# A gated linear attention with an MLP: gates loaded with each chunk's steps turned by one row, and the carried angle added on VectorE

## The chip, the core and the metric

The kernel runs on one core of a Trainium2 chip. The metric is the device time of one execution in microseconds, as the median of several runs. The engines of the core work side by side and wait for each other by semaphores: TensorE (PE in the profile, PEld for its weight loads), VectorE (DVE), ScalarE (ACT), GpSimd (POOL) and SyncE (SP), which here only issues DMA transfers.

## What is computed

A recurrence over 768 steps for 4 batches and 8 heads of 48 channels. Each channel has a complex gate, cut to a magnitude of at most 0.999; the state decays and turns by it and takes in the outer product of key and value; the output is the query times the real part of the state. The result, as 3072 rows of 384, goes through h = x w_in, g = h cos h, g w_out with 2048 inner columns.

```python
mag = np.sqrt(a_re * a_re + a_im * a_im)
scale = np.minimum(mag, 0.999) / (mag + 1e-06)
a_re_n, a_im_n = (a_re * scale, a_im * scale)
for t in range(S):
    ar, ai = (a_re_n[:, :, t, :, None], a_im_n[:, :, t, :, None])
    new_re = ar * S_re - ai * S_im
    new_im = ar * S_im + ai * S_re
    kv = np.einsum('bhd,bhe->bhde', k[:, :, t], v[:, :, t])
    S_re, S_im = (new_re + kv, new_im)
    y[:, :, t] = np.einsum('bhd,bhde->bhe', q[:, :, t], S_re)
x = y.transpose(0, 2, 1, 3).reshape(B * S, H * D)
h = x @ w_in
out = (h * np.cos(h)) @ w_out
```

## The kernel before

The sequence is cut into chunks of C = 128 steps: six to a batch (NCH), 24 in all (N), numbered n. Two chunks with the index i = 0, 1 make a group (G = 2), so there are 12 groups (NG), numbered g, and n = 2g + i. Within a chunk steps lie on the 128 partitions and the 384 numbers of all heads (DM) along the row.

For each group the gates go through these steps. `load` (L543) brings re, im, k, q and v from HBM, one transfer on SP's queue for each tensor and chunk; a row of a transfer is one head of one step, 48 floats or 192 bytes. re, im, k and q have one buffer each, so the gates of group g + 1 can be fetched only when group g has read its own for the last time. `log_steps` (L695) makes the logarithm of the magnitude (tile lg) and the tangent of half the angle (tile tan). `p_powers` (L736) sums lg over the steps of a chunk with a matmul against `sums`, a triangle of ones (result lgs), and takes Exp of it and of its negative. `p_even` and `p_apply` (L748, L771) correct these powers and multiply them into k and q; `p_even` also sends the chunk's last row out to HBM and back with columns on partitions (row, end), which `p_end` (L764) reads. `g_angle` (L783) is the Arctan, in place on tan. `g_phase` (L788) sums the angles over the steps with a matmul against `turns` (the triangle divided by pi); unless the chunk is the first of a batch, a second matmul against `last` (zero but for a last row of ones) adds the last row of the chunk before. The whole turns are then taken off by ScalarE and VectorE (a cast to integer and a subtraction), so that tan now holds phases. `g_trig` and `g_stack` (L801, L812) make sines, cosines and the rotated keys and queries (ks, qs), and `f_transpose` (L824) turns them into kT and qT by way of HBM (tr, moved).

`chunks` (L1011) holds the attention proper: scores (sc), the causal mask (atm), the state (sp, state), the output (yp, yT), and `f_xt` (L931), which moves yT through HBM (x) into xT for the MLP and is followed by the load of v. `first` (L1021) is the product with w_in and its activation (hp, gate, junk); `second` (L1024) the product with w_out (op, ot).

The order is written down by hand. `weave` (L971) takes lists of steps, each with a stretch of the interval 0 to 1, spreads a list's steps evenly over its stretch and runs all in that order. All matmuls and all ScalarE functions that need a table are chained in this order; the other instructions are put in order by the framework's scheduler. In the steady loop (L1090) group n's scores stand beside group n - 1's second product; the log steps of group n + 1 stand at the start, followed by the request for the gates of group n + 2 (L1006); the running sums and Arctan of group n + 1 at 0.38 to 0.4, its phases at 0.49 to 0.51, its keys at 0.52 to 0.7 and group n's first product from 0.56 on. Groups 0 and 1 are arranged apart ahead of the loop, and PEG = 2 (L541) marks the first group of the other way to transpose. The start is ordered by hand too: the gates of group 0 are the first transfers, and POOL fetches the weights only when these are there (L1046). The weights arrive as float64 and are rewritten as float32 while the loop fills up; some are fetched a second time later for a check (`guard`, L614).

Of the kernel before, what the change touches and what calls it, by code (L numbers as in the profile page):

```python
# [18 lines left out]
ALU = mybir.AluOpType  # L19
# [467 lines left out]
def fast_path(ctx, tc, q, k, v, a_re, a_im, moe_w_in, moe_w_out, out, least, odd, wide):  # L487
# [6 lines left out]
    nc = tc.nc  # L494
    B, H, S, D = q.shape
    DM, DF = moe_w_in.shape
    C = 128
    NCH = S // C
    G = 2
    N = B * NCH  # L500
    NG = N // G
# [17 lines left out]
    pm = ctx.enter_context(tc.tile_pool(name="pm", bufs=3, space=PSUM))  # L519

    step_np = np.arange(C)
    sums_np = (step_np[:, None] <= step_np[None, :]).astype(np.float32)
    last_np = np.zeros((C, C), np.float32)
    last_np[C - 1] = 1.0

    def constant(array, name):
        t = consts.tile(list(array.shape), F32, name=name)
        nc.scalar.dma_start(out=t, in_=nc.inline_tensor(array, name=name + "_const").ap())
        return t

    def scalar_tile(value, name):
        t = consts.tile([C, 1], F32, name=name)
        nc.vector.memset(t, value)
        return t

    X = [dict() for _ in range(NG)]
# [4 lines left out]
    PEG, PER = 2, 1  # L541

    def load(g, names, i=None):  # L543
        for name in names:
            ap = {"re": a_re, "im": a_im, "q": q, "k": k, "v": v}[name]
            if name not in X[g]:
                X[g][name] = ld.tile([C, G, H, D], F32, tag=name, name=name,
                                     bufs=2 if name == "v" else 1)
            for i_ in range(G) if i is None else (i,):
                b, c = divmod(g * G + i_, NCH)  # L550
                nc.sync.dma_start(
                    out=X[g][name][:, i_],
                    in_=ap[b].rearrange("h (c p) d -> p c h d", p=C)[:, c])

    for names in ("re", "im"), ("k", "q"), "v":
        for i in range(G):
# [2 lines left out]
    sums = constant(sums_np, "sums")  # L559
    turns = constant(sums_np * np.float32(1.0 / math.pi), "turns")  # L560
    last = constant(last_np, "last")
    causal = constant(sums_np * np.float32(0.25), "causal")
    tiny_b = scalar_tile(TINY, "tiny_b")
    one_b = scalar_tile(1.0, "one_b")
    half_pi_b = scalar_tile(math.pi / 2.0, "half_pi_b")
# [65 lines left out]
    def chain(ins, engine="scalar"):  # L631

        if engine in tail:
            behind(ins, tail[engine])
        tail[engine] = ins
# [22 lines left out]
    vector, scalar = Ordered(nc.vector, "vector"), Ordered(nc.scalar, "scalar")  # L658

    def matmul(out, **kw):  # L660
        chain(nc.tensor.matmul(out, **kw), "tensor")  # L661
# [16 lines left out]
    def special(func, **kw):  # L678
        preload(tables[func])
        chain(nc.scalar.activation(func=func, **kw))  # L680

    def flat(t):
        return t.rearrange("p g h d -> p (g h d)")

    def temp(tag, bufs=1):
        return gt.tile([C, G * DM], F32, tag=tag, name=tag, bufs=bufs)

    def spans(g):

        return [(i, 1) for i in range(G)] if g == 0 else [(0, G)]  # L690

    def cut(t, i, n):
        return (flat(t) if len(t.shape) == 4 else t)[:, ds(i * DM, n * DM)]
# [42 lines left out]
    def p_powers(g, i):  # L736

        x = X[g]
        if i == 0:
            x["P"], x["Q"] = x["lg"], temp("Q")  # L740
            x["row"] = rows_d.tile([G * DM], F32, tag="row", name="row")
            x["end"] = ft.tile([D2, G * H], F32, tag="end", name="end")
        ps = pa.tile([C, DM], F32, tag="a", name="lgs")
        matmul(ps, lhsT=sums, rhs=cut(x["lg"], i, 1), start=True, stop=True)
        special(out=cut(x["P"], i, 1), in_=ps, func=AF.Exp)
        special(out=cut(x["Q"], i, 1), in_=ps, func=AF.Exp, scale=-1.0)

    def p_even(g, i, n):  # L748


        x = X[g]
        u = cut(x["mag"], i, n)
        P, Q = cut(x["P"], i, n), cut(x["Q"], i, n)
        vector.scalar_tensor_tensor(out=u, in0=Q, scalar=HUGE, in1=P, op0=ALU.min, op1=ALU.mult)
        for t in P, Q:
            vector.scalar_tensor_tensor(out=t, in0=u, scalar=3.0, in1=t,
                                        op0=ALU.subtract, op1=ALU.mult)
        row = x["row"][ds(i * DM, n * DM)]
        nc.sync.dma_start(out=row, in_=P[C - 1:C].rearrange("o x -> (o x)"))
        end = x["end"][:, ds(i * H, n * H)]  # L760
        for a in range(2):
            nc.sync.dma_start(out=end[ds(a * D, D)], in_=row.rearrange("(x d) -> d x", d=D))
# [8 lines left out]
    def p_apply(g, i, n):  # L771
        x = X[g]
        P, Q, u = (cut(x[name], i, n) for name in ("P", "Q", "mag"))
        vector.tensor_tensor(out=Q, in0=cut(x["k"], i, n), in1=Q, op=ALU.mult)
        vector.tensor_tensor(out=u, in0=cut(x["q"], i, n), in1=P, op=ALU.mult)

    def g_prod(g, i, n):
        for one in range(i, i + n):
            p_powers(g, one)
        p_even(g, i, n)  # L780
        p_apply(g, i, n)

    def g_angle(g, i, n):  # L783

        at = cut(X[g]["tan"], i, n)
        special(out=at, in_=at, func=AF.Arctan)

    def g_phase(g, i):  # L788

        x, n = X[g], g * G + i  # L790
        ps = pa.tile([C, DM], F32, tag="a", name="phs")
        first = n % NCH == 0
        matmul(ps, lhsT=turns, rhs=cut(x["tan"], i, 1), start=True, stop=first)
        if not first:
            prev = cut(X[(n - 1) // G]["tan"], (n - 1) % G, 1)
            matmul(ps, lhsT=last, rhs=prev, start=False, stop=True)
        ph = cut(x["tan"], i, 1)
        scalar.copy(out=ph.bitcast(I32), in_=ps)
        vector.tensor_tensor(out=ph, in0=ps, in1=ph.bitcast(I32), op=ALU.subtract)
# [181 lines left out]
    def each(step, g):  # L981
        return [lambda i=i, n=n: step(g, i, n) for i, n in spans(g)] if 0 <= g < NG else []

    def keys(g):

        if not 0 <= g < NG:
            return
        for i, n in spans(g):
            yield lambda i=i, n=n: g_trig(g, i, n)
            yield lambda i=i, n=n: (g_stack(g, i, n), p_end(g, i, n))  # L990
            for name in "kT", "qT":
                if g >= PEG:
                    yield lambda i=i, n=n, name=name: f_transpose(g, i, n, name)
# [2 lines left out]
        return [lambda hh=hh: f_turn(g, i, name, hh) for hh in range(2)]  # L996

    def prods(g):
        yield from each(g_prod, g)
        if 0 <= g and g + 1 < NG:  # L1000
            yield lambda: load(g + 1, ("k", "q"))

    def logs(g):
        yield from each(g_log, g)
        if 0 <= g and g + 1 < NG:
            yield lambda: load(g + 1, ("re", "im"))  # L1006

    def phases(g):
        return [lambda i=i: g_phase(g, i) for i in range(G)] if 0 <= g < NG else []

    def chunks(g):  # L1011
        for n in range(g * G, g * G + G):
            for hh in range(2):
                yield lambda n=n, hh=hh: f_scores(n, hh)
            yield lambda n=n: f_state(n)
            yield lambda n=n: f_out(n)
        yield lambda: f_xt(g)
        if g + 2 < NG:
            yield lambda: load(g + 2, ("v",))

    def first(g):  # L1021
        return [lambda jp=jp: mm1(g, jp) for jp in range(NJ // 2)]

    def second(g, i):  # L1024
        return [lambda j0=j0: mm2(g, i, j0, 4) for j0 in range(0, NJ, 4)] if 0 <= g else []

    def convert(parts):
        return [lambda dst=dst, src=src: weight(dst, src)() for dst, src in parts]
# [19 lines left out]
    early = [weight(dst, src) for dst, src in into[:RAW]]  # L1048
# [3 lines left out]
    one, two = (log_steps(0, i, 1) for i in range(2))  # L1052
# [19 lines left out]
    for t in (turned(0, 0, "kT") + turned(0, 0, "qT") + early[:1]  # L1072
# [6 lines left out]
                             lambda: load(2, ("v",))]):  # L1079
        t()  # L1080
    weave((logs(1), 0.0, 0.1), (convert(into[RAW:]), 0.0, 0.5),
          (first(0), 0.2, 1.0), (prods(1), 0.55, 0.57), (each(g_angle, 1), 0.58, 0.6),
          (phases(1), 0.7, 0.8), (keys(1), 0.8, 0.9), (convert(back[:4]), 0.5, 1.0))
    over = [t for i in range(G) for name in ("kT", "qT") for t in turned(1, i, name)]
    weave((convert(back[4:]), 0.0, 0.3), (second(0, 0), 0.0, 0.65), (over, 0.2, 0.6),
          (logs(2), 0.3, 0.31), (chunks(1), 0.7, 1.0), (prods(2), 0.85, 0.86),
          (each(g_angle, 2), 0.86, 0.87))
    weave((second(0, 1), 0.0, 0.35), (phases(2), 0.0, 0.1), (keys(2), 0.1, 0.4),
          (first(1), 0.4, 1.0))
    for n in range(2, NG):  # L1090
        weave((logs(n + 1), 0.0, 0.02), (chunks(n), 0.0, 0.36), (second(n - 1, 0), 0.0, 0.38),
              (prods(n + 1), 0.38, 0.39), (each(g_angle, n + 1), 0.39, 0.4),
              (second(n - 1, 1), 0.4, 0.56), (phases(n + 1), 0.49, 0.51),
              (keys(n + 1), 0.52, 0.7), (first(n), 0.56, 1.0),
              (guarded(n - 1, per) if n > 3 else [], 0.1, 0.9))
    weave((second(NG - 1, 0) + second(NG - 1, 1), 0.0, 1.0))
    assert not guards
# [68 lines left out]
```

## Time and profile before

| | |
|---|---|
| median of 3 runs | 721.38 us (721.3 to 722.37) |
| profiled execution | 718.55 us |
| its span, first to last instruction | 716.7 us |
| granted TensorE clock, mean | 0.987 |
| PE busy in 143.4 to 582.6 us, the steady part | 438.0 of 439.2 us |
| first use of the gates (lg<-re), groups 0 to 3 | 4.4, 41.1, 83.6, 143.4 us |
| the same for group 11, the last | 582.6 us |
| DMA traffic | 94.73 MB, mean 132 GB/s |

A group line names line, engine and operation, the tile written and those read, the shape and the count; then busy time, the mean of one in ns, and the idle time of the engine ahead of it with what ended it. A timeline line has the start, the time that the merged instructions took, and the same names. All instructions issued through a helper have the helper's line: L661 for matmuls, L651 and L680 for VectorE and ScalarE; so one goes by tile names. SPq and POOLq are the queues that issue DMA transfers; their time is the issue, not the transfer. A windows line has a stretch, its length, each engine's busy time with its count, the PE clock, the mean busy share of the 16 DMA engines, and GB/s.

### The profile page before, as it was taken

To read this page: it belongs to the slowest core of one execution; us is meant where nothing else is said; L and a number is where in the kernel's file an instruction comes from. 1 tells how busy PE (TensorE), PEld (TensorE's weight loads), DVE (VectorE), ACT (ScalarE), POOL (GpSimd) and SP (SyncE) were. 2 spreads that over 40 slices of the span, in tenths; PEclk is the share of its full clock that TensorE was granted. 3 is DMA by queue.
4 is the path that set the end of the run, shared out by engine and by line. 5 is a ranking of instruction groups with operands and counts; after the bars stand their busy time and mean duration, and the time that the engine had idled before them with its cause. 6 is when DMAs were issued, how large, how long until landed. Compare 5 with 4: busy or idle time off the path is not lost.

```text
span 716.7 us, 9385 instructions
## 1 busy us (share of the span) xinstructions
PE 688.3 (96%) x3614; PEld 524.4 (73%) x3614; DVE 393.8 (55%) x548; ACT 386.3 (54%) x690; POOL 26.1 (4%) x45
## 2 busy tenths in 40 slices
PE   6786999999999999999999999999999999999995
PEld 5675776876876876876886876876886786786773
DVE  4889987255455563663663664654645655631110
ACT  6778873564564574484483583474474375342330
POOL 1012000000000000000000000000000000000000
PEclk9979999999999999999999999999999999999998
DMA  9678626625725745646646655556665572272000
GB/s 265 131 226 265 167 56 160 139 55 123 176 49 129 177 133 122 162 138 143 161 137 145 149 145 122 148 155 133 156 154 133 146 163 56 88 173 70 12 0 28
DMA packets 231730, 94.73 MB, mean 132 GB/s; under 512 B 207982, under 2 KB 220145, under 8 KB 231676
## 3 DMA queue, kind: packets, MB, share of 16 engines
q1 hardware_dynamic: 225324, 68.55, 43.5%
q0 software_dynamic: 5632, 25.17, 10.3%
q8 instruction: 30, 0.49, 0.3%
q10 hardware_dynamic: 720, 0.33, 0.2%
q14 instruction: 24, 0.20, 0.1%
HBM read 69.22 MB, written 24.81 MB: 131 GB/s over the span
## 4 chain that ended last, share of the span: by engine, by line
PE 81%; DMA 3%; DVE 3%; SPq 1%; ACT 1%; issue 0%; DVEq 0%
PE op L661 34%; PE hp L661 28%; PE sc L661 6%; PE yp L661 5%; PE phs L661 3%; PE sp L661 3%; DMA qT<-moved 2%; PE lgs L661 2%; DVE w_out L651 1%; SPq L837 1%; DMA raw<-in_moe_w_out_dram 1%; DVE ks L651 0%; DVE qs L651 0%; DMA moved<-tr 0%; DVE tr L651 0%
## 5 line engine op out<-in xcount | busy, mean ns | idle before, releaser
L661 PE MATMUL op<-w_out,gate 128*128 128x384 f32 x768 | 262.8, 489 | 0.7 <-DVE w_out L651 0.7
L661 PE MATMUL hp<-xT,w_in 128*128 128x256 f32 x1152 | 254.3, 382 | 3.9 <-ACT junk L651 3.3
L661 PEld LDWEIGHTS hp<-xT,w_in 128*128 128x128 f32 x1152 | 220.7, 192 | 38.1 <-ACT junk L651 3.7
L661 PEld LDWEIGHTS op<-w_out,gate 128*128 128x128 f32 x768 | 142.3, 190 | 95.1 <-issue 3.7
L651 DVE TENSOR_TENSOR gate<-hp,gate 128x512 f32<-128x512 f32 x96 | 65.5, 683 | 135.4 <-ACT gate L680 135.4
L651 ACT ACTIVATE junk<-hp 128x512 bf16<-128x512 f32 x96 | 57.2, 596 | 81.7 <-DVE gate L651 81.6
L680 ACT ACTIVATE gate<-hp,half_pi_b 128x512 f32<-128x512 f32 x96 | 65.5, 684 | 41.6 <-PE hp L661 41.6
L661 PEld LDWEIGHTS sc<-qT,kT 96*128 96x128 f32 x384 | 47.6, 192 | 11.0 <-issue 4.0
L651 ACT COPY yT<-yp 48x512 f32<-48x512 f32 x44 | 25.4, 577 | 52.7 <-PE yp L661 52.0
L661 PE MATMUL sc<-qT,kT 96*128 96x128 f32 x384 | 49.3, 277 | 2.7 <-DMA qT<-moved 0.9
L651 DVE SCALAR_TENSOR_TENSOR mag<-Q,lg 128x768 f32<-128x768 f32 (+1 forms) x13 | 11.6, 894 | 66.6 <-ACT Q L680 66.6
L651 ACT CAST tan<-phs 128x384 int32<-128x384 f32 x24 | 11.5, 481 | 64.6 <-PE phs L661 64.6
L651 DVE TENSOR_TENSOR atm<-sc,causal 128x512 f32<-128x512 f32 x48 | 32.9, 686 | 19.3 <-PE sc L661 19.3
L651 ACT ACTIVATE ot<-op 128x384 f32<-128x384 f32 x24 | 11.6, 483 | 48.6 <-PE op L661 48.6
L676 ACT ACT_TABLE_LOAD x26 | 33.4, 1283 | 3.5 <-issue 3.1
L661 PE MATMUL yp<-atm,v 128*48 128x128 f32 x352 | 33.5, 277 | 0.0
L651 DVE TENSOR_TENSOR tan<-phs,tan 128x384 f32<-128x384 f32 x24 | 13.4, 557 | 30.9 <-ACT tan L651 30.9
L661 PE MATMUL sp<-v,ks 128*96 128x48 f32 x320 | 29.6, 245 | 0.0
L661 PE MATMUL yp<-qT,state 96*48 96x128 f32 x304 | 29.6, 272 | 0.0
L661 PEld LDWEIGHTS sp<-v,ks 128*96 128x96 f32 x320 | 29.4, 165 | 0.3 <-issue 0.2
L661 PE MATMUL phs<-tan,turns 128*128 128x384 f32 x48 | 19.6, 492 | 4.3 <-ACT tan L680 4.3
L661 PEld LDWEIGHTS yp<-atm,v 128*48 128x48 f32 x352 | 19.3, 122 | 5.6 <-issue 3.3
(93 smaller groups left out, 677.7 us busy)
## 6 DMA issues: line engine op xcount, KB each, us to landing
moved<-tr SPq DMA_DIRECT2D x20, 768.0 KB
raw<-in_moe_w_in_dram POOLq DMA_DIRECT2D x16, 768.0 KB, 6.1
raw<-in_moe_w_out_dram POOLq DMA_DIRECT2D x16, 768.0 KB, 5.1
kT<-moved SPq DMA_DIRECT2D x40, 192.0 KB
qT<-moved SPq DMA_DIRECT2D x10, 768.0 KB
re<-in_a_re_dram SPq DMA_DIRECT2D x24, 192.0 KB
im<-in_a_im_dram SPq DMA_DIRECT2D x24, 192.0 KB
k<-in_k_dram SPq DMA_DIRECT2D x24, 192.0 KB
```

Source lines behind the costliest of these rows:

```text
L651: ins = getattr(self.engine, op)(**kw)
L661: chain(nc.tensor.matmul(out, **kw), "tensor")
L676: chain(nc.scalar.preload_act_table_set(table))
L680: chain(nc.scalar.activation(func=func, **kw))
L837: nc.sync.dma_start(out=X[g][name][:, ds(i * H, n * H), q4], in_=moved[q4])
```

## The change

The gates are loaded with each chunk's steps turned by one row: partitions 0 to 126 get steps 1 to 127, and partition 127 gets step 0, in a transfer of its own. The triangles for the sums (`sums`, `turns`) are turned in the same way, so the sums come out in the old order; the causal mask keeps the old triangle. Step 0's angle then lies on the same partition as the last row of the chunk before, so a VectorE instruction on the last 32 partitions can add the carried angle to it (`g_carry`, with a column `carry` that is pi on the last partition and 0 elsewhere) ahead of the matmul with `turns`; the matmul with `last` stays for groups 0 and 1. Group 0 sends the single rows from GpSimd's queue, the others from SP's. `prods` is split into its steps, takes in Arctan and the carry of the group's first chunk, and stands at 0.22 to 0.24 of the steady loop; phases and keys have new stretches.

```diff
-    sums_np = (step_np[:, None] <= step_np[None, :]).astype(np.float32)
+    causal_np = (step_np[:, None] <= step_np[None, :]).astype(np.float32)
+    sums_np = np.roll(causal_np, -1, axis=0)
     last_np = np.zeros((C, C), np.float32)
     last_np[C - 1] = 1.0
+    carry_np = np.where(step_np == C - 1, np.float32(math.pi), np.float32(0.0))[:, None]
...
-            for i_ in range(G) if i is None else (i,):
-                b, c = divmod(g * G + i_, NCH)
-                nc.sync.dma_start(
-                    out=X[g][name][:, i_],
-                    in_=ap[b].rearrange("h (c p) d -> p c h d", p=C)[:, c])
+            b, c = divmod(g * G + (i or 0), NCH)
+            one, n = i or 0, G if i is None else 1
+            steps = ap[b].rearrange("h (c p) d -> p c h d", p=C)[:, ds(c, n)]
+            tile_ = X[g][name][:, ds(one, n)]
+            if name in ("re", "im"):
+                (nc.gpsimd if g == 0 else nc.sync).dma_start(out=tile_[C - 1:C], in_=steps[0:1])
+                steps, tile_ = steps[1:C], tile_[0:C - 1]
+            for i_ in range(n):
+                nc.sync.dma_start(out=tile_[:, i_], in_=steps[:, i_])
...
+    carry = constant(carry_np, "carry")
+    causal = constant(causal_np * np.float32(0.25), "causal")
...
+    def before(n):
+        return cut(X[(n - 1) // G]["tan"], (n - 1) % G, 1)
+
+    def g_carry(g, i):
+        n, some = g * G + i, ds(C - 32, 32)
+        if g >= PEG and n % NCH:
+            head = cut(X[g]["tan"], i, 1)[some]
+            vector.scalar_tensor_tensor(out=head, in0=before(n)[some], scalar=carry[some],
+                                        in1=head, op0=ALU.mult, op1=ALU.add)
...
-        first = n % NCH == 0
-        matmul(ps, lhsT=turns, rhs=cut(x["tan"], i, 1), start=True, stop=first)
-        if not first:
-            prev = cut(X[(n - 1) // G]["tan"], (n - 1) % G, 1)
-            matmul(ps, lhsT=last, rhs=prev, start=False, stop=True)
+        early = g < PEG and n % NCH
+        if i:
+            g_carry(g, i)
+        matmul(ps, lhsT=turns, rhs=cut(x["tan"], i, 1), start=True, stop=not early)
+        if early:
+            matmul(ps, lhsT=last, rhs=before(n), start=False, stop=True)
...
     def prods(g):
-        yield from each(g_prod, g)
-        if 0 <= g and g + 1 < NG:
+        if not 0 <= g < NG:
+            return
+        for i in range(G):
+            yield lambda i=i: p_powers(g, i)
+        yield lambda: g_angle(g, 0, G)
+        yield lambda: g_carry(g, 0)
+        yield lambda: (p_even(g, 0, G), p_apply(g, 0, G))
+        if g + 1 < NG:
             yield lambda: load(g + 1, ("k", "q"))
...
-              (prods(n + 1), 0.38, 0.39), (each(g_angle, n + 1), 0.39, 0.4),
-              (second(n - 1, 1), 0.4, 0.56), (phases(n + 1), 0.49, 0.51),
-              (keys(n + 1), 0.52, 0.7), (first(n), 0.56, 1.0),
+              (prods(n + 1), 0.22, 0.24),
+              (second(n - 1, 1), 0.4, 0.56), (phases(n + 1), 0.4, 0.52),
+              (keys(n + 1), 0.49, 0.66), (first(n), 0.56, 1.0),
```

More of the change, by code (lines that the diff above doesn't have):

```diff
@@ L561, in fast_path @@
     last = constant(last_np, "last")
-    causal = constant(sums_np * np.float32(0.25), "causal")
+    carry = constant(carry_np, "carry")
+    causal = constant(causal_np * np.float32(0.25), "causal")
     tiny_b = scalar_tile(TINY, "tiny_b")
@@ L775, in p_apply @@
         vector.tensor_tensor(out=u, in0=cut(x["q"], i, n), in1=P, op=ALU.mult)
[L777 to L781, printed above, removed]
     def g_angle(g, i, n):
@@ L1081, in fast_path @@
     weave((logs(1), 0.0, 0.1), (convert(into[RAW:]), 0.0, 0.5),
-          (first(0), 0.2, 1.0), (prods(1), 0.55, 0.57), (each(g_angle, 1), 0.58, 0.6),
+          (first(0), 0.2, 1.0), (prods(1), 0.55, 0.58),
           (phases(1), 0.7, 0.8), (keys(1), 0.8, 0.9), (convert(back[:4]), 0.5, 1.0))
@@ L1085, in fast_path @@
     weave((convert(back[4:]), 0.0, 0.3), (second(0, 0), 0.0, 0.65), (over, 0.2, 0.6),
-          (logs(2), 0.3, 0.31), (chunks(1), 0.7, 1.0), (prods(2), 0.85, 0.86),
-          (each(g_angle, 2), 0.86, 0.87))
+          (logs(2), 0.3, 0.31), (chunks(1), 0.7, 1.0), (prods(2), 0.85, 0.87))
     weave((second(0, 1), 0.0, 0.35), (phases(2), 0.0, 0.1), (keys(2), 0.1, 0.4),
```

## The prediction

> **What bounds the kernel now.** I read the page's busy table and chain first, then the groups by form, then the timelines of PE and SP over one steady group, and last the DMA issues and one window. Page, parts 1 and 4:
>
> ```profile
> span 716.7 us, 9385 instructions
> PE 688.3 (96%) x3614; PEld 524.4 (73%) x3614; DVE 393.8 (55%) x548; ACT 386.3 (54%) x690; POOL 26.1 (4%) x45
> PE 81%; DMA 3%; DVE 3%; SPq 1%; ACT 1%; issue 0%; DVEq 0%
> ```
>
> TensorE is the bound: it works through one fixed row of matmuls and the chain lies on it for 81% of the span. The matmul that the change removes, and the nearest row to the instruction that it adds, in the groups by form:
>
> ```profile
> L661 PE MATMUL phs<-tan,last 128*128 128x384 f32 x40 | 16.3, 489 | 0.5 <-DVE tan L651 0.5
> L651 DVE SCALAR_TENSOR_TENSOR mag<-Q,lg 128x384 f32<-128x384 f32 x2 | 1.1, 550 | 0.0
> ```
>
> PE's timeline around the second phase sum of one group:
>
> ```profile
> 336.99 0.81 PE L661 MATMUL phs<-tan,turns 128*128 128x384 f32 x2
> 337.64 0.81 PE L661 MATMUL phs<-tan,last 128*128 128x384 f32 x2
> 338.28 2.74 PE L661 MATMUL op<-w_out,gate 128*128 128x384 f32 x8
> 340.86 20.88 PE L661 MATMUL hp<-xT,w_in 128*128 128x256 f32 x96
> ```
>
> A float32 product is two records, so 40 are 20 calls, and one call moves PE on by 338.28 - 337.64 = 0.64 us. From 340.86 on PE spends 20.9 us on hp, which needs xT. Now SP's queue in the same group, where I think the change is decided:
>
> ```profile
> 318.17 1.03 SPq L551 DMA_DIRECT2D re<-in_a_re_dram  x2
> 321.32 0.99 SPq L551 DMA_DIRECT2D im<-in_a_im_dram  x2
> 324.53 0.37 SPq L551 DMA_DIRECT2D v<-in_v_dram  x1
> 325.36 0.93 SPq L935 DMA_DIRECT2D x<-yT  x2
> 328.98 0.64 SPq L939 DMA_DIRECT2D xT<-x  x1
> 331.85 0.25 SPq L759 DMA_DIRECT2D row<-lg  x1
> 334.15 1.10 SPq L762 DMA_DIRECT2D end<-row  x2
> 346.22 3.06 SPq L834 DMA_DIRECT2D moved<-tr  x2
> ```
>
> The gate loads (re, im) are issued ahead of x, xT, row, end and moved of the same group, all on one queue. ACT's use of those gates, and what 192-byte packets cost, from ACT's timeline and from a window in which the only DMA traffic is loads of 192-byte rows (48 floats):
>
> ```profile
> 362.37 0.83 ACT L704 ACTIVATE lg<-re 128x768 f32<-128x768 f32 x1
> ...
> 372.76 0.19 ACT L651 ACTIVATION_READ_ACCUMULATOR rs<-re 128x1 f32 x1
> 372.97 1.02 SPq L551 DMA_DIRECT2D re<-in_a_re_dram  x2
> ```
>
> ```profile
> 6.00:8.00 2.00, 2.00 (x11) 2.00 (x11) 0.47 (x2) 1.27 (x3) 0.72 (x2) 1.00 1.38 219
> ```
>
> The last column is GB/s: 16 engines x 192 B / 219 GB/s = 14.0 ns per packet and engine. The column ahead of it (1.38, busy share of the 16 engines) over the same rate gives 19.4 ns, an upper bound, since packets overlap. A gate load is 128 rows x 8 heads = 1024 packets, 64 per engine, 0.9 us. The gates issued at 318-322 are wanted at 362.37: about 41 us of slack.
>
> **What the Trainium skill says.** (1) "DMA: Bandwidth & Descriptors", section "Why a DMA increments its semaphore by 16 and not by 1": a DMA runs on the largest k of at most 16 engines that divides both sides' slowest dimension; it names 127 partitions as k = 1, on the lowest-numbered engine. No load of the kernel before has such a shape, so no run shows it; all its big transfers have 48, 96 or 128 rows. (2) Same page, "Queues, rings and completion order": each engine takes a queue's descriptors in ring order, and switches between queues by packet. The trace fits: four v loads behind the first weight loads took SP 11.9 us (7.79 to 19.65) instead of about 4. (3) "TensorE: Matmul & The Clock Gate", "What's actually happening": after an idle window of 3.4 us the array runs at half clock until it has been busy that long, an estimated 1.7 us a restart. The trace agrees in kind: PEclk is 0.88 in 41.1:83.6, where PE is busy for 35.1 of 42.5 us.
>
> **The change part by part.**
>
> *Removed.* The product with last goes for n from 4 to 23 except 6, 12, 18: 17 calls x 0.64 = 10.9 us of PE. This is the whole possible gain, 1.5%.
>
> *Added on DVE.* 17 products of 32 partitions x 384. Bounds: 0.17 us (the 96x16 row) to 0.55 us (the 128x384 row); I take 0.55, so 9.4 us on an engine with 45% idle. For i = 1 it stands ahead of the phase matmul: in the group shown, first phs at 333.77, subtraction done at 335.69, carry about 336.3, second phs at 336.99: 0.6 us to spare, because 8 op matmuls lie between. If that cover went, a group would lose up to 1 us.
>
> *Moved.* lgs, its four Exp, table load, Arctan, the five DVE products, row, two end and the k and q loads go from 0.38 to 0.22 of the weave, ahead of or beside the x transfers on SP. The carry for i = 0 waits for Arctan (4 x 0.49 + 1.28 + 0.84 = 4.1 us after lgs); behind it on DVE stands state, for which yp<-qT,state on PE waits. 16 sp and 8 op matmuls (4.1 us) cover it; bounds nothing to 1.7 us in each of the six groups 4, 5, 7, 8, 10, 11. I take nothing.
>
> *Added constants and row loads.* One 512-byte constant on ACT's queue and, at the start, four one-row loads on POOL, idle until 7.28: nothing. Later two one-row loads a group on SP at about 0.4 us, 16 packets each: nothing beside what follows.
>
> *The 127-row loads.* By (1) each puts 127 x 8 = 1016 packets on one engine: 1016 x 14.0 = 14.2 us, four a group 57 us (upper bound 79; below 57 only if it isn't k = 1). That exceeds the 41 us of slack, and by (2) everything behind it on SP's queue has its sixteenth on that engine and waits too: x, xT, row, end, moved. So in a group, from lg<-re (call it L): to the re issue 10.6 us (372.97 - 362.37); drain 57; two guard loads of the weights in between, 2.3 us each per engine (queue q0: 10.3% of 716.7 / 32), 5; x, xT, row, end, p_end, last phs and 8 op matmuls until hp, about 10 (325.36 to 329.62, 3 to land, the rest as at 337.57 to 340.86); hp 20.9 and the next L; restart 2. Sum 106, in place of 55.
>
> *The sum.* Start: the four first loads in series end at 2 + 57 + 2 = 61 instead of 7.25, +54. Group 1: its im goes out at 19.8 + 54 = 74, drains behind v and four weight loads by 107; row and end behind it 112; k and q 115; re 28.5 plus 5 of weights, landing 2, and k and q among them: L1 = 153 (before 41.1). L2: 13 (54.08 - 41.10) + 57 + 15 of weights + 5 for row and end + 5.4 (end at 78.21, lg at 83.57) = 95: 248. L3: 17.6 (101.21 - 83.57) + 57 + 5 + 10 + 21 = 111: 359. L4 to L11: 8 x 106 = 848: about 1205. After L11 no gates are loaded: 716.7 - 582.6 = 134, less 1.3 for two removed calls: span 1338. The profiled execution took 718.55, 1.85 over its span, and the median of 721.38 is 2.8 above it: 1342 us.
>
> **Rivals.**
> - *One engine, but no one waits behind it* (x and moved get past the gates). Then the busiest engine bounds a group: 57 + 30 (0.62 of 54 us in 308.4:362.4, less the old gates' 3.6) = 87; 359 + 8 x 87 + 133 + 4.7 = 1193. Against: SP issues re and im first, and one ring serves the queue.
> - *The loads are spread over all engines after all* (the other side: faster). It decides from the drain of four loads: under 41 us nobody waits. Price: 0.9 us a load as now, so only the 10.9 us gain is left: 721.4 - 10.9 = 710.5. For it: no odd-row load in the trace contradicts it; against it: the page's explicit 127.
> - *Spread, and the carry costs what the matmul saved*: 1 us in each of 10 groups: about 720.5, no change. Against: the 0.6 us of spare above.
>
> **How the numbers follow.** Forecast 0.81, one engine without blocking 0.10, spread 0.07, spread and eaten 0.02. Likeliest: 1342. Its own range: 14.0 to 19.4 ns adds at most 12 x 22 = 262; partial overlap takes off up to 150: 1190 to 1600. With the first rival 1170 to 1600, which leaves out the two spread cases and about a tenth of the rest. A measurement here tells 0.2% (1.4 us) from no change. Slower: 0.81 + 0.10 = 0.91, and 0.005 of the last; faster 0.075; same 0.01.
>
> **What would show it.** Right: SP's issues of re and im last tens of us; about 24 x 2 x 1016 fewer packets are spread; hp's idle before it is ended by DMA xT, about 50 us a group; PE's share near 50%; the DMA share of the 16 engines stays low while one is full. The phs<-tan,last count falls from 40 to 6, and 17 new products stand on DVE near 0.55 us. Wrong: re and im issue in about 1 us as before, groups keep their 54 us, and the time falls by about 11 us.

## The result, and the profile after

The changed kernel takes 1212.42 us (median of 4 runs, 1210.68 to 1212.65) against 721.47 us for the kernel before: a ratio of 1.6795, interval 1.6766 to 1.6824. The span of its profiled execution is 1208.9 us. Forecast were 1342 us, between 1170 and 1600.

The page of the changed kernel, its parts 1 and 4:

```profile
span 1208.9 us, 9368 instructions
PE 704.2 (58%) x3580; PEld 535.8 (44%) x3580; DVE 404.1 (33%) x565; ACT 389.2 (32%) x690; POOL 27.8 (2%) x49
...
PE 46%; SPq 25%; DMA 22%; ACT 3%; DVE 3%; issue 1%; DVEq 0%; ACTq 0%
PE hp L670 21%; SPq L561 15%; PE op L670 14%; DMA row<-lg 13%; SPq L558 8%; PE sc L670 3%; PE yp L670 3%; DMA xT<-x 3%; DMA x<-yT 3%; DMA im<-in_a_im_dram 2%; PE sp L670 2%; DMA raw<-in_moe_w_out_dram 1%; PE lgs L670 1%; DVE tan L660 1%; PE phs L670 1%
```

No engine does much more than before (PE's busy time has grown by 16 us); the span has grown by 492 us, nearly all of it waiting. A quarter of the chain is now SP's queue and another fifth transfers. L561 and L558 are the two `dma_start` calls of `load`. On PE most of the idle time (351 of 505 us) stands ahead of hp, on VectorE the largest part (406 us) ahead of end; the first number after the second bar is the idle time ahead of the group, then what ended it. The changed kernel, then the kernel before:

```profile
L670 PE MATMUL hp<-xT,w_in 128*128 128x256 f32 x1152 | 275.7, 404 | 350.7 <-DMA xT<-x 350.1
L660 DVE TENSOR_SCALAR end<-end 96x16 f32<-96x16 f32 x12 | 2.1, 171 | 406.3 <-DMA end<-row 406.3
```

```profile
L661 PE MATMUL hp<-xT,w_in 128*128 128x256 f32 x1152 | 254.3, 382 | 3.9 <-ACT junk L651 3.3 <-ACT xT L651 0.6
L651 DVE TENSOR_SCALAR end<-end 96x16 f32<-96x16 f32 x12 | 2.1, 176 | 11.2 <-DMA end<-row 11.1
```

SP's queue of one steady group tells why:

```profile
519.72 0.68 SPq L558 DMA_DIRECT2D re<-in_a_re_dram  x1
520.45 12.11 SPq L561 DMA_DIRECT2D re<-in_a_re_dram  x2
532.66 11.86 SPq L558 DMA_DIRECT2D im<-in_a_im_dram  x1
544.56 12.04 SPq L561 DMA_DIRECT2D im<-in_a_im_dram  x2
556.71 11.81 SPq L768 DMA_DIRECT2D row<-lg  x1
568.62 1.01 SPq L561 DMA_DIRECT2D k<-in_k_dram  x2
570.38 0.91 SPq L771 DMA_DIRECT2D end<-row  x2
571.38 1.10 SPq L561 DMA_DIRECT2D q<-in_q_dram  x2
572.57 1.27 SPq L950 DMA_DIRECT2D x<-yT  x2
...
577.19 0.36 SPq L954 DMA_DIRECT2D xT<-x  x1
```

An issue that took half a microsecond takes 12. The one-row transfers, 0.25 us for row in the group shown of the kernel before, take 11.8 when they stand behind a 127-row load: SP gets rid of a transfer only when the one ahead has nearly drained. From the first long issue to the end of row's it is 48.1 us for four loads. A window in that stretch (the last two columns are the mean busy share of the 16 DMA engines and GB/s):

```profile
523.00:567.00 44.00, 20.01 (x97) 12.31 (x96) 7.47 (x11) 5.81 (x10) 0.00 (x0) 0.76 0.08 16
```

0.08 of sixteen is about one engine, and 192 B at 16 GB/s are 12 ns a packet. The chain of waits over the same group runs through SP's queue and the transfer of row to hp. (Its step from the carry into an issue is inferred, and no sign that the carry held the queue up: that issue had begun at 532.66, before the carry.)

```profile
535.77 0.63 DVE tan L660
536.40 8.12 SPq L558
544.56 0.41 SPq L561
545.01 11.58 SPq L561
...
556.71 13.65 DMA row<-lg
...
573.41 3.76 DMA x<-yT
577.19 3.55 DMA xT<-x
580.79 23.80 PE hp L670 x96
```

PE had done everything that stands ahead of hp in its order at 543.0; it stands still until 580.8. In the kernel before the same stretch had no pause.

### The profile page after: what moved, and what is told of

It is laid out like the page before. It is cut to its first block, busy times and chain, and to the rows that moved or that the text cites. A ratio compares the mean times of both kernels' runs of the same rounds, so it can differ in the third digit from the quotient of the medians.

```text
span 1208.9 us, 9368 instructions
## 1 busy us (share of the span) xinstructions
PE 704.2 (58%) x3580; PEld 535.8 (44%) x3580; DVE 404.1 (33%) x565; ACT 389.2 (32%) x690; POOL 27.8 (2%) x49
## 4 chain that ended last, share of the span: by engine, by line
PE 46%; SPq 25%; DMA 22%; ACT 3%; DVE 3%; issue 1%; DVEq 0%; ACTq 0%
PE hp L670 21%; SPq L561 15%; PE op L670 14%; DMA row<-lg 13%; SPq L558 8%; PE sc L670 3%; PE yp L670 3%; DMA xT<-x 3%; DMA x<-yT 3%; DMA im<-in_a_im_dram 2%; PE sp L670 2%; DMA raw<-in_moe_w_out_dram 1%; PE lgs L670 1%; DVE tan L660 1%; PE phs L670 1%
## 5 line engine op out<-in xcount | busy, mean ns | idle before, releaser
L670 PE MATMUL hp<-xT,w_in 128*128 128x256 f32 x1152 | 275.7, 404 | 350.7 <-DMA xT<-x 350.1
L670 PEld LDWEIGHTS hp<-xT,w_in 128*128 128x128 f32 x1152 | 234.8, 205 | 394.0 <-DMA xT<-x 355.6
L689 ACT ACTIVATE sin<-tan 128x768 f32<-128x768 f32 (+1 forms) x13 | 10.3, 793 | 344.2 <-DVE tan L660 344.2
L670 PEld LDWEIGHTS sc<-qT,kT 96*128 96x128 f32 x384 | 48.1, 192 | 7.5 <-ACT qT L660 1.2
L670 PE MATMUL sc<-qT,kT 96*128 96x128 f32 x384 | 48.8, 275 | 0.9 <-ACT qT L660 0.9
L670 PE MATMUL lgs<-lg,sums 128*128 128x384 f32 x48 | 18.5, 504 | 46.6 <-DVE lg L660 46.6
L660 DVE TENSOR_TENSOR lg<-lg,tan 128x768 f32<-128x768 f32 (+1 forms) x13 | 11.7, 897 | 80.0 <-ACT tan L714 80.0
L660 ACT COPY yT<-yp 48x512 f32<-48x512 f32 x44 | 25.4, 577 | 24.3 <-PE yp L670 23.3
L713 ACT ACTIVATE lg<-re 128x768 f32<-128x768 f32 (+1 forms) x13 | 10.2, 787 | 68.0 <-DMA re<-in_a_re_dram 68.0
L670 PEld LDWEIGHTS lgs<-lg,sums 128*128 128x128 f32 x48 | 8.4, 195 | 49.9 <-DVE lg L660 46.9
```

The lines of the kernel that those rows point to most:

```text
L660: ins = getattr(self.engine, op)(**kw)
L713: chain(nc.scalar.activation(out=m2, in_=re, func=AF.Square))
```

## The experiments

Theory A is the forecast: the 127-row shape puts a load on one engine, and the transfers behind it on the queue wait. Theory B says that the moved steps or the carry cost by themselves; theory C that any odd shape or any cut is slow. The last forecast rival, that one engine is used but nobody waits behind it, is tested by the number of engines below. Each ratio is against the kernel before, run beside.

**The shape alone, in the kernel before.** Label e2_old_127. Steps aren't turned, nothing else is touched.

```diff
+            if name in ("re", "im"):
+                (nc.gpsimd if g == 0 else nc.sync).dma_start(out=tile_[C - 1:C],
+                                                             in_=steps[C - 1:C])
+                steps, tile_ = steps[0:C - 1], tile_[0:C - 1]
```

> The kernel before with nothing changed but the shape of the gate loads: rows 0 to 126 in one transfer and row 127 in another, steps not turned, last still added by a matmul, old order. Theory A: within 30 us of the changed kernel, 1200 to 1240 us, since 17 calls are more by 11 us but lie where PE waits anyway. Theory B: clearly less, under 1150 us, the rest being due to the new order. Idle before hp ended by DMA xT near 40 us a group in A.

Measured 1172.66 us (2 runs), ratio 1.6265 (1.6201 to 1.6328). SP's queue in one group:

```profile
418.69 12.01 SPq L558 DMA_DIRECT2D re<-in_a_re_dram  x2
430.81 11.95 SPq L554 DMA_DIRECT2D im<-in_a_im_dram  x1
442.81 12.16 SPq L558 DMA_DIRECT2D im<-in_a_im_dram  x2
455.07 12.30 SPq L940 DMA_DIRECT2D x<-yT  x2
...
470.22 0.36 SPq L944 DMA_DIRECT2D xT<-x  x1
```

The shape alone makes more than nine tenths of the loss: 0.63 of 0.68. But the time lies 40 us below the changed kernel, outside of what A expected. Here x stands directly behind the gates, and xT goes out 15.3 us after the last gate issue ends (454.97 to 470.22); in the changed kernel row, k, end and q stand between, and it is 20.6 us (556.60 to 577.19). By these two timelines the sooner running sums cost some 5 us a group with the gate loads in the way (no run has 127 rows in the new order without the carry, so this is argued and not shown by itself). The steady stretch from the logs of group 3 to those of group 11 is 720.2 us here and 757.1 there.

**Two and four engines.** Labels e5_two_engines and e6_four_engines. The changed kernel with its 127 rows cut in another place: 122 = 2 x 61, 124 = 4 x 31.

```diff
-            for i_ in range(n):
-                nc.sync.dma_start(out=tile_[:, i_], in_=steps[:, i_])
+            turned = name in ("re", "im")
+            for lo, hi in ((0, 122), (122, C - 1)) if turned else ((0, C),):
+                for i_ in range(n):
+                    nc.sync.dma_start(out=tile_[lo:hi, i_], in_=steps[lo:hi, i_])
```

> The changed kernel, its 127 rows cut as 122 and 5: 122 = 2 x 61, so the large part should run on two engines, 488 packets each. If the rule of the largest divisor up to 16 holds and an engine takes 11.8 ns a packet: SP's issue of a large part lasts about 5.8 us, four drain in 24 instead of 48 us, a group takes 9.8 + 24 + 12.3 + 24.4 = 70.5 us and the kernel 900 to 950 us. If cutting alone or any shape that isn't 128 rows made it slow: near 1200 us. If two engines are enough to stay under the 41 us of slack and only the gates' own return counts: about 715 us.

> As e5_two_engines with 124 and 3 rows: 124 = 4 x 31, four engines, 248 packets each. By the divisor rule an issue lasts about 2.9 us, a group takes 9.8 + 12 + 12.3 + 24.4 = 58.5 us in place of 53, the kernel 760 to 790 us. If only the gates' own return counts: about 715 us.

Measured 925.82 us, ratio 1.2833 (1.2783 to 1.2884), and 794.61 us, ratio 1.1015 (1.0972 to 1.1057), 2 runs each; the first lies in the range that was expected, the second 4.6 us above it. The re and im issues of one group, first with two engines, then with four; a line merges two large and two small parts:

```profile
372.74 12.02 SPq L563 DMA_DIRECT2D re<-in_a_re_dram  x4
385.56 11.98 SPq L563 DMA_DIRECT2D im<-in_a_im_dram  x4
```

```profile
310.07 6.31 SPq L563 DMA_DIRECT2D re<-in_a_re_dram  x4
317.19 6.35 SPq L563 DMA_DIRECT2D im<-in_a_im_dram  x4
```

The profile doesn't name the engine of a packet, but the rate shows how many work: one made 16 GB/s in the window above, and windows inside these drains have 33 GB/s with 122 rows and 65 with 124 (the last column):

```profile
375.00:383.00 8.00, 8.00 (x64) 5.68 (x63) 6.65 (x9) 4.63 (x8) 0.00 (x0) 1.00 0.16 33
312.00:316.00 4.00, 4.00 (x26) 2.76 (x24) 3.12 (x6) 3.79 (x7) 0.00 (x0) 1.00 0.32 65
```

**Sixteen engines.** Label e1_spread: the same with 112 and 15 rows.

> All of the change, but the 127 rows of a gate load go as 112 and 15 rows, which divide over 16 and 15 engines (7 or 8 rows of 8 packets an engine), at the price of one more transfer per load. Theory A, the one engine of the 127-row loads is the whole loss: the issues last 0.4 to 0.6 us again, a group takes 53 us, and what is left is the gain of 17 calls x 0.64 = 10.9 us less 1 to 2 us at the start: 710 to 713 us. Theory B, the moved running sums or the carry cost too: above 718 us, with new idle time of PE before yp or phs. Theory C, any odd-row load is slow however it is cut: above 800 us.

Measured 711.67 us (6 runs), ratio 0.987 (0.9846 to 0.9893). With it the row of engine counts is complete. The third column is from the start of the first large re issue to the end of the last im issue (for one engine to the end of row's, which drains the last load); a group is an eighth of the time from the logs of group 3 to those of group 11. The 16 of the last row is the divisor, not a count from the profile; what the profile shows is that no issue waits there any more:

| rows of the large part | engines | four loads, us | a group, us | median, us |
|---|---|---|---|---|
| 127 | 1 | 48.1 | 94.6 | 1212.4 |
| 122 | 2 | 24.8 | 71.6 | 925.8 |
| 124 | 4 | 13.5 | 60.5 | 794.6 |
| 112 | 16 | 5.0 | 53.6 | 711.7 |

A group gets shorter almost us for us with the drain: 23.0 for 23.3, then 11.1 for 11.3, then 6.9 for 8.5. So A holds, and the rival in which nobody waits behind the gates falls: with four engines the gates are back long before the 41 us are over, and a group still pays 7 us, because x stands behind them. Of these 7 us 4.7 are waiting (PE idle for 37.3 us in the eight groups), and 2.3 are slower matmuls after the pause (PE busy for 446.6 us in the eight groups, 428.5 in e1_spread). C falls too.

**The order alone, and the carry in the old order.** Labels e3_order_only (the kernel before with the new `prods` and the new stretches, without the carry) and e4_spread_old_order (e1_spread with the old ones).

```diff
-              (prods(n + 1), 0.38, 0.39), (each(g_angle, n + 1), 0.39, 0.4),
-              (second(n - 1, 1), 0.4, 0.56), (phases(n + 1), 0.49, 0.51),
-              (keys(n + 1), 0.52, 0.7), (first(n), 0.56, 1.0),
+              (prods(n + 1), 0.22, 0.24),
+              (second(n - 1, 1), 0.4, 0.56), (phases(n + 1), 0.4, 0.52),
+              (keys(n + 1), 0.49, 0.66), (first(n), 0.56, 1.0),
```

> The kernel before with the new order alone (running sums and Arctan at 0.22, phases and keys as in the change), gates loaded as before and last still added by matmuls. Theory A: no PE work removed, 719 to 724 us. Theory B: slower, 725 us or more, with idle time of PE. A gain over 3 us would say that the sooner keys take the stall at sc (DMA qT) away.

> As e1_spread with 112 and 15 rows and the carry on VectorE, but in the order of the kernel before (running sums at 0.38, phases at 0.5). Theory A: 710 to 714 us, the order is worth under 3 us. If the order is what makes room for the carry: 716 us or more, with PE waiting at phs for the carry (its chain cast, subtraction, carry is about 0.6 us longer than before).

Measured 716.71 us (7 runs), ratio 0.9943 (0.9921 to 0.9964), and 713.38 us (6 runs), ratio 0.9902 (0.9876 to 0.9929). The order is a small gain, not a cost: B falls, and so does the "same" of A for e3_order_only. Scores (sc) in the kernel before, in e3_order_only and in e1_spread, groups by form:

```profile
L661 PE MATMUL sc<-qT,kT 96*128 96x128 f32 x384 | 49.3, 277 | 2.7 <-DMA qT<-moved 0.9 <-ACT qT L651 0.9 <-issue 0.7
```

```profile
L661 PE MATMUL sc<-qT,kT 96*128 96x128 f32 x384 | 48.9, 275 | 0.9 <-ACT qT L651 0.9
```

```profile
L672 PE MATMUL sc<-qT,kT 96*128 96x128 f32 x384 | 48.8, 275 | 0.9 <-ACT qT L662 0.9
```

The wait for the transfer of qT is gone, because the keys come sooner (e4_spread_old_order, in the old order, has it again with 1.3 us), but it is not the whole gain of the order. In the steady stretch PE is busy for 437.9 of 439.1 us in the kernel before and for all of the 436.9 us with the order alone: of the 2.3 us gained 1.2 are idle time, and the other 1.0 is busy time, for which the runs show no reason. The steady stretch (logs of group 3 to logs of group 11) adds up: 439.1 us before, 436.9 with the order alone (-2.3), 430.7 with the carry alone (-8.5), 428.5 with both (-10.7). Between these logs lie the phases of groups 3 to 10, with 13 removed calls; 13 x 0.64 us is 8.3.

**Another queue.** Label e7_pool_queue: the changed kernel with the 127-row loads of groups 2 to 11 on GpSimd's queue.

```diff
+            pool = name in ("re", "im") and g >= PEG
-                nc.sync.dma_start(out=tile_[:, i_], in_=steps[:, i_])
+                (nc.gpsimd if pool else nc.sync).dma_start(out=tile_[:, i_], in_=steps[:, i_])
```

> The changed kernel with the 127-row loads of groups 2 to 11 issued from GpSimd's queue instead of SP's, so that x, row and moved of SP's queue aren't behind them in one ring. If the four loads of a group still share one engine: the gates' own return bounds a group, 10 + 48 + about 22 of other work on that engine = 80 us, 1050 to 1110 us in all. If GpSimd's queue picks another engine for each load, or spreads one: four loads side by side take 12 us or less, nobody waits, and only the start (loads of groups 0 and 1, still on SP) keeps its loss, L2 at about 190: 790 to 830 us. If what counts is that a gate load of such a shape is slow as such: no change, near 1210 us.

Measured 1382.34 us (2 runs), ratio 1.9162 (1.9089 to 1.9235): slower than the change itself, and outside of all three ranges. POOL's timeline of one group:

```profile
608.66 6.69 POOL L562 DMA_DIRECT2D re<-in_a_re_dram  x1 [7.71 <-ACT rs L661]
631.93 6.68 POOL L562 DMA_DIRECT2D re<-in_a_re_dram  x1 [16.58 <-issue]
660.62 6.66 POOL L562 DMA_DIRECT2D im<-in_a_im_dram  x1 [22.01 <-DMA kT<-moved]
683.79 6.66 POOL L562 DMA_DIRECT2D im<-in_a_im_dram  x1 [16.50 <-issue]
```

and the DMA issues of its page with KB and the median time to landing:

```profile
re<-in_a_re_dram POOLq DMA_DIRECT2D x20, 190.5 KB, 24.9
im<-in_a_im_dram POOLq DMA_DIRECT2D x20, 190.5 KB, 22.9
```

A load of this shape takes GpSimd 6.7 us to issue and some 24 us to land, and the next one starts no sooner than 23 us after it. The second im load of this group, issued at 683.79, lands by the median of 22.9 us at about 706.7, 98 us after the first re load was issued, and there ACT's wait for it ends:

```profile
706.64 0.84 ACT L715 ACTIVATE tan<-im 128x768 f32<-128x768 f32 x1 [43.35 <-issue]
```

A group takes 108.5 us. So the mechanism of the first case held, the gates' own return bounds a group, but at 108.5 us instead of 80; whether the loads share one engine here the profile doesn't show. In the trace's packet records a load has become 46 packets of 4224 bytes and one of 768, which are its 195072 bytes, with 690 packets of 88 bytes beside them (1840, 40 and 27600 over 40 loads), where SP's queue has 1016 of 192 bytes. Why the next load starts only 23 us later is left open. Leaving SP's queue was no cure; changing the shape was.

**The start.** In e1_spread the logs of group 1 start at 48.2 us against 41.1 before, so 7 us of the gain are lost there. (All times of stages are from one profiled execution of each kernel.) Label e8_late_turn keeps groups 0 and 1 unturned, with the old triangles beside the turned ones; GpSimd's queue fetches the turned ones and the column `carry`.

```diff
-            if name in ("re", "im"):
+            turned = name in ("re", "im") and g >= PEG
+            if turned:
...
-        matmul(ps, lhsT=turns, rhs=cut(x["tan"], i, 1), start=True, stop=not early)
+        matmul(ps, lhsT=turns if g < PEG else late_turns, rhs=cut(x["tan"], i, 1), start=True, stop=not early)
```

> As e1_spread, but the gates of groups 0 and 1, whose carry is a matmul anyway, are loaded unturned in one transfer of 128 rows and summed with the old triangles; the turned triangles are two further constants, fetched by GpSimd's queue. e1_spread reached the logs of group 1 at 48.2 us against 41.1 us before, so theory A expects these 7 us back: 703 to 707 us, ratio about 0.977. If the start's delay in e1_spread has another cause (the placement of ScalarE's work): 710 to 713 us as there.

Measured 710.18 us (5 runs), ratio 0.9842 (0.9817 to 0.9868); the logs of group 1 start at 43.6, those of group 3 at 147.7 (150.8 in e1_spread, 143.4 before). About 3 us of the 7 came back, not all, and the whole time lies in the second case of what was expected: 1.5 us under e1_spread, with intervals that overlap. Label e9_old_start puts back two more things, the place of these constants and the old order of group 1:

```diff
+        if g < PEG:
+            yield lambda: (p_even(g, 0, G), p_apply(g, 0, G))
+            yield lambda: load(g + 1, ("k", "q"))
+            yield lambda: g_angle(g, 0, G)
+            return
         yield lambda: g_angle(g, 0, G)
         yield lambda: g_carry(g, 0)
...
     early = [weight(dst, src) for dst, src in into[:RAW]]
+    carry = constant(carry_np, "carry", nc.gpsimd)
+    late_sums = constant(late_np, "late_sums", nc.gpsimd)
+    late_turns = constant(late_np * np.float32(1.0 / math.pi), "late_turns", nc.gpsimd)
```

> As e8_late_turn, with two things put back at the start: the carry column and the two turned triangles are fetched by GpSimd's queue behind the first weights instead of beside the first gates (there the gates of chunk 1 were used 1.1 us later than before), and group 1 keeps the old order of its running sums and Arctan (the new one took 44.9 us from the logs of group 1 to those of group 2 in the order alone, against 42.5 before). If both count, the logs of group 3 start at 143 to 145 us instead of 147.7 and the kernel takes 705 to 708 us, ratio about 0.979; if the start is set by something else: 710 us as e8_late_turn.

Measured 708.95 us (5 runs), ratio 0.9827 (0.9803 to 0.9852), the lowest time of this study, though above the range that was hoped for, and its interval overlaps that of e8_late_turn. The logs of group 1 start at 42.0, 1.6 us sooner than in e8_late_turn; those of group 2 follow 44.6 us later in spite of the old order, and by the logs of group 3 nothing is left of the 1.6 (147.6 against 147.7). So the order's half of the guess was wrong. The 44.9 us of e3_order_only against 42.5 before, on which it rested, go along with the clock instead: between these two logs the granted clock was 0.81 in e3_order_only and in e9_old_start and 0.88 in the kernel before. The last 4 us at the start (147.6 against 143.4) stay unexplained; up to 2.8 of them may be mere spread between executions, since the profiled execution of the kernel before lies that much under its median.

## Why the prediction was right, and where its sizes were off

- *What bounds the kernel.* Right: with the loads spread, the carry in the old order takes 8.5 us off the steady stretch, where 13 of the 17 removed calls lie, at the forecast's price 8.3. That the whole time of e1_spread comes so near to the forecast of that rival, 711.67 against 710.5 us, is partly luck: the order gains some 2 us more, and the start loses some 7 (logs of group 3 at 150.8 us instead of 143.4).
- *The 127-row loads on one engine, and all of SP's queue behind them.* Right, shown by the 12 us issues, by the rate that doubles and doubles again with 122 and 124 rows, and by the row of engine counts. One detail differs: the prediction had the transfers behind wait in the ring, and the timeline shows them wait at SP to be issued. The term of the sum that was mis-sized is the drain: four loads were put at 57 us plus 5 for the weights' check in between, and they take 48.8 (519.72 to 568.52). A packet was priced at 14.0 ns, from a window in which all 16 engines worked at 219 GB/s; one engine alone needs 12.0 us / 1016 = 11.8 ns. And the check's loads don't lie in between: GpSimd issues them at 511.44, and by the packet records they are done at 518.0, ahead of the first long gate issue at 520.45. What they would add to a drain that they meet isn't shown.
- *The group.* 106 us forecast, 94.6 measured: logs to re issue 9.8 instead of 10.6, drain 48.8 instead of 62, from there to hp 12.3 instead of 10, hp and the next logs 24.4 instead of 22.9. The slower first matmuls after the pause are there: hp's 96 records take 23.80 us where they took 20.88, 2.9 more, where the estimate was 1.7 and 2 were put in. The granted clock is 0.50 for the first 5.7 us of hp (580.79 to 586.52), and half of 5.7 is 2.9.
- *The sum.* Logs of group 1 at 133.0 (153), of group 2 81.4 later (95), of group 3 105.3 later (111), eight groups 757 (848), the tail 132.1 (133). In the eight groups the drain and the check's loads make 13 us too many each, and the other terms together some 2 to 3 too few; that is 91 of the 129 us. The other 39 lie in the start, whose four drains were priced in the same way; how they divide wasn't worked out.
- *The moved steps at nothing.* Half wrong. Alone they gain 2.3 us in the steady part, about half of it idle time. With the slow loads the changed kernel takes 37 us longer there than e2_old_127, which the timelines put down to row, k, end and q standing between the gates and x. The prediction put "x, xT, row, end, p_end" at 10 us whatever their order.
- *The carry at 0.55 us, hidden.* Hidden, yes: in the changed kernel PE's waits at phs that VectorE ended come to 1.2 us in all. Its size is 0.617, above the upper bound of 0.55 that was taken from the 128-partition row.
- *Rivals.* One engine without blocking falls with e5_two_engines and e6_four_engines. "Spread" was the right price for a change that wasn't made. "Spread and eaten by the carry" falls with e4_spread_old_order.

## What to carry to other kernels

Ask of every transfer how many DMA engines its row count lets it use, and cut rows so that the large part divides by 16 (here 112 and a rest of 15 instead of 127): the page of the Trainium skill "DMA: Bandwidth & Descriptors" (section "Why a DMA increments its semaphore by 16 and not by 1") gives the rule, and 127, 122, 124 and 112 rows behaved as it says (16, 33 and 65 GB/s for the first three; with 112 rows four parts were issued in 2.05 us). A slow transfer isn't judged by its own slack: what decides is what stands behind it on the same queue, and here that was paid nearly microsecond for microsecond. Price a resource at the load under which it will run: a rate read where sixteen engines work at once (14.0 ns a packet) wasn't the rate of one alone (11.8).

## What the runs showed of the hardware that wasn't expected

One DMA engine alone moves 192-byte packets at 11.8 ns each, faster than the 14.0 ns per engine where all sixteen are busy, although the packet records are longer than that in both cases, 15.0 ns alone and some 19 with all busy: they overlap. SP's queue takes about one such load ahead, so the issue of the next transfer, however small, lasts as long as the load ahead of it (row: 11.81 us).

The carry on 32 partitions x 384 takes longer than the same kind of instruction on 128 partitions x 384, from the groups by form of the changed kernel and of the one before:

```profile
L660 DVE SCALAR_TENSOR_TENSOR tan<-tan,carry 32x384 f32<-32x384 f32 x17 | 10.5, 617 | 1.1 <-ACT tan L689 0.6
```

```profile
L651 DVE SCALAR_TENSOR_TENSOR mag<-Q,lg 128x384 f32<-128x384 f32 x2 | 1.1, 550 | 0.0
```

One difference between the two is that the carry's factor is a column of the tile, and mag's a constant; that this makes the 67 ns wasn't tried. And a 127-row load from GpSimd's queue is slower (24 us to land, the next one 23 us later at the soonest) than one from SP's queue (12 us by the issues behind it).
